# Attention, a mixture of experts and a feed-forward layer on one core: the route of five token tiles, the last gate, one V transfer and two narrowing operations change places

## The chip, the core and the metric

The kernel runs on one core of a Trainium2 chip. The metric is the device time of one execution in microseconds; the time of a kernel is the median of its runs. The profile is of one further execution.

## What is computed

Three layers follow one another in float32 (cut to what matters):

```python
scores = q @ k.T / 8 + bias            # 2 batches, 8 heads, 576 positions, head size 64
attn   = softmax(scores)               # bias: a small MLP of log-distances, per head
x      = (attn @ v) as [1152, 512]
logits = x @ w_gate;  e = argmax(logits);  gate = softmax(logits)[e]
# each token goes to its expert e; an expert takes the first 288 tokens in order
y      = gate * (relu(x @ w1[e]) @ w2[e])      # w1 [8,512,1024], w2 [8,1024,512]
h      = y @ w_in;  out = (h * cos(h)) @ w_out # [512,2048], [2048,512]
```

The kernel keeps float32 accuracy in the later layers by splitting each operand in a high and a low part, so that three matmuls stand for one. The weights of the last layer arrive as 64-bit numbers and are "narrowed" to float32 on the chip.

## The kernel before

**Attention.** The 1152 tokens are nine blocks of 128 rows: tiles 0 to 3 and 5 to 8, and one joint block for tiles 4 and 9 (64 rows of each batch). A block has four steps, one for each pair of heads, so there are 36 steps (`ns`), written out by `step_of(n)` (L882). In step n TensorE makes the scores of step n+1, transposes the exponentials of step n and multiplies those of step n-1 with V (`emit_pv`, L464); VectorE adds the bias to the scores of step n+1 (`emit_sum`, L411); ScalarE does the exponentials. The products are transposed back (`emit_nat`) and normalised into token rows (`emit_nrm`, L507) two steps later.

The bias is made in 36 groups, each by a few matmuls, an eviction, and a DMA (`bias_part`, L329) that spreads a group over the rows of a block's bias. Group n+10 is made in step n and sent in step n+1. The scores of step 8, summed in step 7, are the first of row block 1 and need its groups 8 to 15; group 15 is sent in step 6. The V pieces of batch 1 are loaded at the end of the steps listed in `V_AT` (L52, `load_step`, L839), one for each pair of heads; the last is first read by the values product of step 8. All these DMAs are issued from one queue, that of SyncE (SP), in the order of the code.

**Narrowing.** Each weight piece of the last layer needs one ScalarE operation and three on VectorE (shift, low, sign; `narrow`, L761); the last of them also issues the fetch of a later piece. `LOWS` (L40) says how many of the VectorE ones each late step takes.

**Gate and route.** When a block is done, `finish_block` (L538) makes its gate in four parts: f1 four matmuls (and a ScalarE or VectorE copy), f2 a transposition and the VectorE operations down to the expert's one-hot row `oh`, f3 an exponential on ScalarE, f4 the gate's value, a memset and an iota on GpSimd. `route(ts)` (L607) counts with small matmuls of the one-hot rows where each token of the tiles `ts` goes, then on VectorE makes the addresses `sl`, and GpSimd scatters the token rows into a buffer in DRAM (`disp`), one indirect DMA for each tile. Tiles 0 to 2 are routed during attention, tiles 3 to 7 in one call, tiles 8 and 9 last (`last_route`). The result of the counting lies where `late_ps` (L530) says.

**Expert 0** begins within step 35. `expert(s, ...)` (L1035) is a generator over eight groups m of the hidden layer:

```python
for k in range(4): ... T.matmul(out=ps, ...)      # 12 matmuls of the first layer, group m
for f in turn.get(m, ()): f()
...                                               # hh, hl, and splits of later weights (L1045 to L1050)
yield
for f in mid.get(m, ()): f()
if m > 0: second(s, m - 1)                        # 12 matmuls of the second layer, group m - 1
for f in side.get(m, ()): f()
```

Work of other parts is hung into `turn`, `mid` and `side` by hand. In the kernel before, `turn[1]` holds `last_but_one` (the transposition and normalisation of step 34), `mid[2]` holds `last_pair` (route of tiles 3 to 7, its matmuls around the same for step 35), `side[1]` the last block's f1, `side[2]` f2 to f4, `side[3]` `last_route` and `second_expert`, the DMA that fetches the second expert's rows from `disp` into `xg` and so waits for all scatters. The lists also hold the fetches of the second expert's weights. The next expert begins with `turned(1)`: TensorE transposes `xg`. Each engine works through its own instructions in the order of the code.

Of the kernel before, what the change touches and what calls it, by code (L numbers as in the profile page):

```python
# [24 lines left out]
E, FF, CAP = 8, 1024, 288  # L25
# [14 lines left out]
LOWS = {27: 1, 28: 2, 29: 2, 30: 1, 31: 1, 32: 2, 35: 3}  # L40
# [6 lines left out]
LATE_FROM = 32  # L47
# [1 line left out]
LATE_B = {34: 1}  # L49
LATE_C = {33: 1, 34: 1, 35: 1, 36: 1}  # L50
FETCH_AT = 1, 2, 4, 5
V_AT = 1, 3, 4, 5  # L52
CHOOSE = (1, 1)

LEAD = 10
# [52 lines left out]
def attention_moe_kernel(  # L108
# [116 lines left out]
    xb, bb, t0, t1 = (banks.tile([128, 512], F32, name=n) for n in ("xb", "bb", "t0", "t1"))  # L225
# [202 lines left out]
    def turn_half(ps, src, r):  # L428

        half = slice(64 * r, 64 * r + 64)  # L430
        T.transpose(ps, src[half], ident[half, half])  # L431
# [63 lines left out]
    def emit_nat(n):  # L495

        b, ib, p = steps[n]
        src = xs_t[b, ib][:, p, :]
        if at_step[0] < PLAIN:
            nat_t[n] = s_of[0][:, :, HS:HS + 64]  # L500
            for r in range(2):
                turn_half(nat_t[n][:, r], src, r)
        else:
            T.transpose(spare[0], src, ident)
            nat_t[n] = two_of(spare[0])

    def emit_nrm(n):  # L507
        b, ib, p = steps[n]
        ps = nat_t.pop(n)
        rz = rz_t[b, ib][:, 2 * p:2 * p + 2]  # L510
        V.tensor_tensor(
            out=xn_t[b, ib][:, 128 * p:128 * p + 128].rearrange("p (h d) -> p h d", h=2), in0=ps,
            in1=rz[:, :, None].to_broadcast([128, 2, D]), op=ALU.mult,
        )
# [10 lines left out]
    own = []  # L525
# [7 lines left out]
    def whole(f):  # L533

        for _ in f() or ():
            pass
# [200 lines left out]
    def go_on(rest_):  # L737
        for g in rest_:
            next(g, None)
# [99 lines left out]
    def load_step(n):  # L839
# [4 lines left out]
        if n == 2:  # L844
            Y.dma_start(out=wgs, in_=wg)
        if n in V_AT:
            load_v(1, (V_AT.index(n),))

# [30 lines left out]
    early_mags, early_lows = [f[0] for f in early_ops], [g for f in early_ops for g in f[1:]]  # L879
    ready, behind = [], []  # L880

    def step_of(n):  # L882

        g, nxt = RUNS.get(n), RUNS.get(n + 1)
        at_step[0] = n
        if n > 1:
            b, ib, p = steps[n - 2]
            if p == NP - 1 and n < SOONER:
                finish_block(b, ib)
                ready.append((b, ib))  # L890

        while ready and n >= ROUTE_FROM:
            tile_done(*ready.pop(0))
        while late and n < LATE_FROM and late[0][0] == -2:
            whole(late.pop(0)[1])
        if 0 < n <= PLAIN:
            emit_exp(n, 1)
        while behind:
            behind.pop(0)()
        if n in MAGS:  # L900
            early_mags.pop(0)()
        hook(n, "first")
        if n + 1 < ns:
            b, ib, p = steps[n + 1]
            j = BLOCKS.index((b, ib))
            for u in range(2):
                emit_qk(n + 1, u)
            if p == int(j == 1) and 0 < j < len(BLOCKS) - 1:
                fetch_q(*BLOCKS[j + 1])
            if n == 0:  # L910
                bias_h(g, quads=(3,))
            emit_exp(n + 1, 0)
        if n == ns - 4:
            aux[0] = V
        hook(n, "start")
        emit_tr(n)
        if n > 1:
            emit_nat(n - 2)
        hook(n, "turned")
        begun = []  # L920
        if n >= PLAIN:
            go_on(run_late(LATE_A.get(n, 0)))
            begun = run_late(LATE_B.get(n, n < LATE_FROM))
        emit_tev(n, 2)
        if g is not None:
            bias_half(g, 0)()
        emit_tev(n, 0)
        emit_tev(n, 1)
        if n < PLAIN:
            begun = run_late(1)  # L930
        e_t.pop(n)
        if nxt is not None:
            bias_h(nxt, quads=(0, 1))
        go_on(begun)
        if n > 1:
            emit_nrm(n - 2)
        if nxt is not None:
            bias_h(nxt, quads=(2, 3))
        for _ in range(LOWS.get(n, 0)):
            early_lows.pop(0)()  # L940
        while held:
            held.pop(0)()
        hook(n, "values")
        if 0 < n:
            emit_rz(n - 1)
            emit_pv(n - 1)
            if PLAIN <= n < ns - 1:
                emit_exp(n + 1, 1)
            emit_xs(n - 1)
        if n == SOONER:  # L950
            b, ib, p = steps[n - 1]
            finish_block(b, ib)
            tile_done(b, ib)
        go_on(run_late(LATE_C.get(n, 0)))
        if g is not None:
            evict = bias_half(g, 1, bb if n > 1 else xb[:, 128:])
            if g == NG - 1:
                evict()
            else:
                behind.append(evict)  # L960
        if n != ns - 2:
            made_up()
        load_step(n)
        while again and again[0][0] <= n:
            fetch_piece(again.pop(0)[1])
        if n in FILL_AT:
            i = FILL_AT.index(n)
            fill_rows(256 * i, min(256, E1 * CAP - 256 * i))
        if 0 <= n - DOUBLE_AT < NP:
            double(n - DOUBLE_AT)  # L970
        for j, at_ in enumerate(OUT_AT):
            if at_ == n:
                fill_out(j)
        hook(n, "end")
# [53 lines left out]

    def last_but_one():
        spare[0] = t1[:, 384:512]  # L1030
        emit_nat(ns - 2)
        emit_rz(ns - 1)
        emit_nrm(ns - 2)

    def expert(s, side, mid={}, turn={}):  # L1035

# [35 lines left out]
    e0_side, e0_mid = {m: [] for m in range(8)}, {}  # L1072
# [32 lines left out]
    emit_xs(ns - 1)  # L1105

    def last_pair():
        g = route(range(3, 8))()
        next(g)
        emit_nat(ns - 1)  # L1110
        emit_nrm(ns - 1)
        go_on([g])

    spare[0] = xb[:, 384:512]
    at_step[0] = ns
# [22 lines left out]
    def ids_of(i):  # L1138
        words = (xg if i < 2 else xs_few[:, None])[:, :, DM].bitcast(I32)
        V.tensor_copy(idn[i][0:words.shape[0], 0:words.shape[1]], words)  # L1140

    def ids_on(i, at_, o):
        n, c = (FEW, 1) if i == 2 else (96, 3)
        for j in range(c):
            T.transpose(xb[0:1, at_ + n * j:at_ + n * j + n], idn[i][0:n, j:j + 1], ident[:n, :n])
        A.activation(out=idrow[:, o], in_=xb[0:1, at_:at_ + n * c], func=AF.Copy)
# [105 lines left out]
        e0_side[m] += [in_e0.pop(0) for _ in range(n)]  # L1252
    f1, f2, f3, f4, last_route = [lambda f=f: whole(f) for f in tail]
    for m, fs in (
        (1, [f1]), (2, [f2, f3, f4]), (3, [last_route, second_expert]), (4, [make_list]), (5, [pick_few]),
    ):
        e0_side[m][0:0] = fs
    e0_mid.update({1: [lambda: ids_of(0)], 2: [last_pair], 6: [lambda: ids_on(0, 128, slice(0, CAP))]})
    for m, (a, c) in enumerate((((0,), (0,)), ((1,), ()), ((), (1,)), ((2,), ()), ((), (2,)), ((3,), (3,)))):
        e0_side[m] += [lambda a=a: fetch_w1(eid[1], a), lambda c=c: fetch_w2(eid[1], c)]  # L1260
    e0_side[6].append(fetch_third)
# [311 lines left out]
```

## Time and profile before

| what | value |
|---|---|
| median of 3 runs | 359.8 us (358.77, 359.80, 360.05) |
| the profiled execution, its own time | 361.18 us |
| its span in the profile | 359.4 us |
| TensorE matmuls busy | 343.7 us, 96% |
| VectorE, ScalarE, GpSimd busy | 82%, 74%, 11% |
| mean granted clock of TensorE | 0.984 of full speed |

All times in rows count from the start of the span. PE is TensorE's matmuls, PEld its weight loads, DVE VectorE, ACT ScalarE, POOL GpSimd, SP SyncE. "out<-in" are the program's tiles (numbers left out: `t` is t0 or t1, `v` v12); wo and wi also lend their room to other data, so `wo` can be the last V piece, a token row or a bias group on its way, and `wi` a V piece or the joint block's bias. In brackets stands how long an engine was idle before the instruction, and what the profile takes for the releaser.

### The profile page before, as it was taken

Reading aid. Unit: us, or ns where it says so; the run is one execution under the profiler, and the core shown is the slowest. Engines: PE = TensorE matmul, PEld = TensorE weight load, DVE = VectorE, ACT = ScalarE, POOL = GpSimd, SP = SyncE. Lnnn points to the kernel's source line nnn. Section 1 sums busy time; section 2 is a strip of 40 time slices with the busy share of each in tenths; the row PEclk is TensorE's granted clock in tenths of the full one; section 3 lists DMA queues with packets and bytes.
Section 4 is the critical chain, followed back from the end, with each engine's and each line's share of the span. In section 5 each row is a group of like instructions: output and inputs, shape, how many; then the busy total and the mean of one; then the engine's idle time right before and its main releaser. Section 6 shows DMA issues by size and latency. Waiting matters only on the chain.

```text
span 359.4 us, 10904 instructions
## 1 busy us (share of the span) xinstructions
PE 343.7 (96%) x4291; PEld 275.5 (77%) x4291; DVE 293.5 (82%) x770; ACT 267.7 (74%) x630; POOL 38.4 (11%) x89
## 2 busy tenths in 40 slices
PE   8989997999999999999999799999999999999992
PEld 6446775777666777777889799978898898898881
DVE  5998785898979987988989879977997887878550
ACT  6879995999988898999844478577877576766660
POOL 3000010010101420210006211300000000000023
PEclk9999998999999999999999989999999999999997
DMA  7799995786986697899348497954233133300003
GB/s 234 194 242 263 217 246 168 234 222 155 279 247 178 215 260 190 258 262 303 96 134 285 106 370 250 289 195 155 57 120 118 64 120 113 118 1 2 0 28 118
DMA packets 47021, 63.85 MB, mean 178 GB/s; under 512 B 5772, under 2 KB 30476, under 8 KB 46962
## 3 DMA queue, kind: packets, MB, share of 16 engines
q1 hardware_dynamic: 45666, 60.24, 57.5%
q0 software_dynamic: 1152, 2.48, 2.0%
q8 instruction: 35, 0.57, 0.7%
q10 hardware_dynamic: 144, 0.36, 0.3%
q14 instruction: 24, 0.20, 0.2%
HBM read 41.08 MB, written 11.47 MB: 146 GB/s over the span
## 4 chain that ended last, share of the span: by engine, by line
PE 44%; issue 29%; DVE 8%; ACT 5%; DMA 4%; POOL 1%; SPq 0%; POOLq 0%; DVEq 0%; ACTq 0%
PE sa L473 8%; PE bb L350 8%; PE hp L1042 5%; PE sb L406 5%; PE t L431 4%; PE sa L406 3%; PE t L1022 2%; DVE e L414 2%; ACT e L423 2%; PE sb L431 1%; DMA xg<-disp 1%; PE bb L1022 1%; PE ac L1022 1%; ACT et L454 1%; POOL out_dram L1389 1%
## 5 line engine op out<-in xcount | busy, mean ns | idle before, releaser
L423 ACT ACTIVATE e<-e,mn 128x576 f32<-128x576 f32 x72 | 56.3, 782 | 16.5 <-DVE mn L414 16.4
L324 DVE TENSOR_SCALAR h<-tt,sml 128x576 f32<-128x576 f32 x121 | 56.9, 515 | 0.1
L454 ACT ACTIVATE et<-t 128x512 f32<-128x512 f32 x72 | 38.9, 597 | 0.0
L350 PE MATMUL bb<-h,sml 128*32 128x288 f32 x400 | 35.5, 420 | 0.1
L431 PEld LDWEIGHTS t<-ident,e 64*128 64x128 f32 x576 | 24.2, 139 | 8.1 <-issue 1.8
L406 PE MATMUL sb<-k,q 64*128 64x288 f32 (+1 forms) x160 | 27.1, 449 | 1.1 <-DVE mn L414 1.0
L1305 PE MATMUL t<-yh,s1h 128*128 128x352 f32 (+1 forms) x88 | 26.8, 305 | 0.0
L1305 PE MATMUL t<-yh,s1l 128*128 128x352 f32 (+1 forms) x88 | 26.7, 303 | 0.0
L1305 PE MATMUL t<-yl,s1h 128*128 128x352 f32 (+1 forms) x88 | 26.5, 302 | 0.0
L431 PE MATMUL t<-ident,e 64*128 64x64 f32 x576 | 25.6, 225 | 0.8 <-ACT e L423 0.8
L356 ACT ACTIVATE wo<-bb,sml 128x288 f32<-128x288 f32 x49 | 24.8, 505 | 0.9 <-PE bb L350 0.8
L406 PE MATMUL sa<-k,q 64*128 64x288 f32 (+1 forms) x160 | 23.7, 405 | 0.0
L1426 ACT ACTIVATE gh<-tn 128x608 fp32r<-128x608 f32 (+2 forms) x19 | 12.0, 631 | 15.1 <-DVE tn L1423 15.0
L473 PE MATMUL sa<-et,wi 128*32 128x128 f32 (+1 forms) x700 | 23.0, 266 | 0.0
L406 PEld LDWEIGHTS sb<-k,q 64*128 64x128 f32 (+1 forms) x160 | 10.5, 174 | 16.2 <-issue 6.2
L1416 DVE TENSOR_TENSOR tn<-tn,kn 128x608 f32<-128x608 f32 (+2 forms) x19 | 13.1, 692 | 11.1 <-ACT kn L1413 11.1
L473 PEld LDWEIGHTS sa<-et,wi 128*32 128x32 f32 (+1 forms) x700 | 19.7, 114 | 2.4 <-DVE mn L414 1.5
L1042 PE MATMUL hp<-xh,s1h 128*128 128x288 f32 x64 | 19.8, 309 | 0.2 <-DVE xl L1016 0.2
L1401 PE MATMUL hp<-s2h,gh 128*128 128x512 f32 x48 | 19.1, 398 | 0.0
L1042 PE MATMUL hp<-xl,s1h 128*128 128x288 f32 x64 | 19.1, 298 | 0.0
L1401 PE MATMUL hp<-s2l,gh 128*128 128x512 f32 x48 | 19.0, 396 | 0.0
L1042 PE MATMUL hp<-xh,s1l 128*128 128x288 f32 x64 | 19.0, 297 | 0.0
(309 smaller groups left out, 993.5 us busy)
## 6 DMA issues: line engine op xcount, KB each, us to landing
keep<-win SPq DMA_DIRECT2D x16, 512.0 KB, 7.0
keep<-wout SPq DMA_DIRECT2D x16, 512.0 KB, 3.5
w1r<-mw SPq DMA_DIRECT2D x12, 512.0 KB, 5.2
w2r<-mw SPq DMA_DIRECT2D x12, 512.0 KB, 7.1
disp<-wo SPq DMA_DIRECT2D x10, 516.0 KB, 6.2
bias<-wo SPq DMA_DIRECT2D x15, 288.0 KB, 5.3
q<-qd SPq DMA_DIRECT2D x8, 512.0 KB, 6.8
k<-kd SPq DMA_DIRECT2D x8, 288.0 KB, 8.2
```

Of the source, the lines that this page charges most:

```text
L324: V.tensor_scalar(out=h, in0=win_, scalar1=col, scalar2=0.0, op0=ALU.add, op1=ALU.max)
L350: T.matmul(out=ps[32 * j:32 * j + 32, :], lhsT=w2s, rhs=h_t[g, j][:, cols], start=True, stop=True)
L356: A.activation(out=ev_t[g][:, cols], in_=ps, func=AF.Copy, scale=rst[:, g:g + 1])
L406: T.matmul(out=ps[a:e, half, 0:HS], lhsT=qt[b, ib][rows_, h, a:e], rhs=kt[c, p][rows_, u, :], start=True, stop=True)
L423: A.activation(out=e_t[n][:, u], in_=e_t[n][:, u], func=AF.Exp, scale=-1.0, bias=mn_t[n][:, u:u + 1], accum_out=z_t[b, ib][:, h:h + 1],)
L431: T.transpose(ps, src[half], ident[half, half])
L454: A.activation(out=et_t[n][:, 0:8, 64 * g:64 * g + 64], in_=halves[g], func=AF.Copy)
L473: T.matmul(out=xo[w * i:w * i + w], lhsT=v_of(c, p, at_, w), rhs=et[:, 4 if j == 4 else 5 * u + j, a:e], start=(j == 4), stop=(j == 3),)
L1022: T.matmul(out=acc[d], lhsT=a[g % 3][:, 128 * d:128 * d + 128], rhs=x[m % 2], start=(m == 0 and i == 0), stop=(m == 7 and i == 2),)
L1042: T.matmul(out=ps, lhsT=a[g % 3][:, k], rhs=x[:, k], start=(k == 0 and i == 0), stop=(k == 3 and i == 2))
L1305: done.append(T.matmul(out=sums(f, i), lhsT=w[f % 3][:, k], rhs=ya[k][x][:, o0 + a:o0 + e], start=(k == 0 and n == 0), stop=(k == 3 and n ...
L1401: T.matmul(out=oacc[t][rows_of(t)], lhsT=x, rhs=b[f % 3], start=(f == 0 and n == 0), stop=(f == 15 and n == 2))
```

## The change

The route of tiles 3 to 7 moves from `last_pair` in group 2 to `last_but_one` in group 1, around the latter's transposition, and its counts go to columns 128 to 256 of bank t1. What is left of `last_pair` moves from `mid[2]` to `side[1]`. f2 to f4 of the last block, its route and the fetch of the second expert's rows move from behind the second-layer product of their group to ahead of it. The last V piece of batch 1 is loaded at the end of step 6 and no more of step 5. In step 32 the two narrowing operations on VectorE come ahead of the normalisation of step 30.

```diff
--- before.py
+++ after.py
@@ -49,7 +49,7 @@
 LATE_B = {34: 1}
 LATE_C = {33: 1, 34: 1, 35: 1, 36: 1}
 FETCH_AT = 1, 2, 4, 5
-V_AT = 1, 3, 4, 5
+V_AT = 1, 3, 4, 6
 CHOOSE = (1, 1)
 
 LEAD = 10
@@ -878,6 +878,10 @@
     early_ops = [narrow(i) for i in range(EARLY)]
     early_mags, early_lows = [f[0] for f in early_ops], [g for f in early_ops for g in f[1:]]
     ready, behind = [], []
+
+    def narrow_on(n):
+        for _ in range(LOWS.get(n, 0)):
+            early_lows.pop(0)()
 
     def step_of(n):
 
@@ -932,12 +936,14 @@
         if nxt is not None:
             bias_h(nxt, quads=(0, 1))
         go_on(begun)
+        if n == LATE_FROM:
+            narrow_on(n)
         if n > 1:
             emit_nrm(n - 2)
         if nxt is not None:
             bias_h(nxt, quads=(2, 3))
-        for _ in range(LOWS.get(n, 0)):
-            early_lows.pop(0)()
+        if n != LATE_FROM:
+            narrow_on(n)
         while held:
             held.pop(0)()
         hook(n, "values")
@@ -1028,9 +1034,14 @@
 
     def last_but_one():
         spare[0] = t1[:, 384:512]
+        own.append(t1[:, 0:384])
+        g = route(range(3, 8))()
+        next(g)
         emit_nat(ns - 2)
         emit_rz(ns - 1)
         emit_nrm(ns - 2)
+        go_on([g])
+        own.pop()
 
     def expert(s, side, mid={}, turn={}):
 
@@ -1105,11 +1116,8 @@
     emit_xs(ns - 1)
 
     def last_pair():
-        g = route(range(3, 8))()
-        next(g)
         emit_nat(ns - 1)
         emit_nrm(ns - 1)
-        go_on([g])
 
     spare[0] = xb[:, 384:512]
     at_step[0] = ns
@@ -1252,10 +1260,10 @@
         e0_side[m] += [in_e0.pop(0) for _ in range(n)]
     f1, f2, f3, f4, last_route = [lambda f=f: whole(f) for f in tail]
     for m, fs in (
-        (1, [f1]), (2, [f2, f3, f4]), (3, [last_route, second_expert]), (4, [make_list]), (5, [pick_few]),
+        (1, [f1, last_pair]), (4, [make_list]), (5, [pick_few]),
     ):
         e0_side[m][0:0] = fs
-    e0_mid.update({1: [lambda: ids_of(0)], 2: [last_pair], 6: [lambda: ids_on(0, 128, slice(0, CAP))]})
+    e0_mid.update({1: [lambda: ids_of(0)], 2: [f2, f3, f4], 3: [last_route, second_expert], 6: [lambda: ids_on(0, 128, slice(0, CAP))]})
     for m, (a, c) in enumerate((((0,), (0,)), ((1,), ()), ((), (1,)), ((2,), ()), ((), (2,)), ((3,), (3,)))):
         e0_side[m] += [lambda a=a: fetch_w1(eid[1], a), lambda c=c: fetch_w2(eid[1], c)]
     e0_side[6].append(fetch_third)
```

## Rows read from the trace of the kernel before

**Rows 1.** The page: busy time of TensorE, and its granted clock in 40 slices.
```profile
PE 343.7 (96%) x4291; PEld 275.5 (77%) x4291; DVE 293.5 (82%) x770; ACT 267.7 (74%) x630; POOL 38.4 (11%) x89
...
PEclk9999998999999999999999989999999999999997
```

**Rows 2.** Windows: stretch, length, busy time by engine, granted clock, DMA share, GB/s.
```profile
45.00:50.00 5.00, 5.00 (x112) 3.88 (x108) 4.31 (x14) 4.39 (x13) 0.00 (x0) 1.00 1.10 250
57.70:61.10 3.40, 3.40 (x54) 2.48 (x50) 2.67 (x9) 2.70 (x9) 0.00 (x0) 0.50 1.00 289
207.90:211.30 3.40, 3.40 (x17) 3.40 (x16) 3.40 (x10) 2.80 (x8) 0.00 (x0) 0.50 1.08 370
```

**Rows 3.** Waits of TensorE, 5 to 64 us: total, times, longest.
```profile
PE sb L431 <- DVE mn L414: 2.3, 1, 2.3
```

**Rows 4.** TensorE's instructions in order of time: start, length, line, operation, idle before.
```profile
23.17 0.76 PE L406 MATMUL sb<-k,q 64*128 64x288 f32 x4 [0.97 <-DVE mn L414]
...
63.45 1.28 PE L473 MATMUL sa<-et,wo 128*32 128x128 f32 x40
...
181.21 0.40 PE L1022 MATMUL t<-hh,s2h 128*128 128x288 f32 x1
...
187.87 0.33 PE L556 MATMUL xb<-ident,wo 128*128 128x128 f32 x1 [0.40 <-DVE jk L634]
...
189.62 0.30 PE L1022 MATMUL t<-hh,s2h 128*128 128x288 f32 x1
...
206.56 0.93 PE L1011 MATMUL hp<-ident,xg 96*128 96x96 f32 x9 [1.85 <-DMA xg<-disp]
```

**Rows 5.** VectorE in order of time: the first sum of step 7.
```profile
56.13 0.76 DVE L414 CUSTOM_DVE_ANT_0 e<-sb,bias 128x576 f32<-128x576 f32 x1 [2.65 <-DMA wi<-wo]
```

**Rows 6.** SP's queue in order of time: the last V piece, bias group 15.
```profile
46.06 0.58 SPq L301 DMA_DIRECT2D wo<-vp  x1
...
49.73 0.53 SPq L331 DMA_DIRECT2D bias<-wo  x1
```

**Rows 7.** DMA issues from 20 to 60 us: count, KB each, median us to landing.
```profile
bias<-wo SPq DMA_DIRECT2D x8, 288.0 KB, 6.6
...
v<-vp SPq DMA_DIRECT2D x2, 320.0 KB, 10.3
```

**Rows 8.** VectorE's instructions in order of time, step 32 and expert 0.
```profile
163.91 0.29 DVE L511 TENSOR_TENSOR wo<-xb,rz 128x128 f32<-128x128 f32 x1 [1.02 <-ACT et L457]
...
181.29 0.45 DVE L1046 SCALAR_TENSOR_TENSOR hl<-hp,hh 128x288 fp32r<-128x288 f32 x1
...
185.69 0.46 DVE L1046 SCALAR_TENSOR_TENSOR hl<-hp,hh 128x288 fp32r<-128x288 f32 x1 [0.89 <-ACT hh L1045]
...
187.62 0.19 DVE L634 TENSOR_TENSOR jk<-xb,oh 128x40 f32<-128x40 f32 x1
...
189.17 0.22 DVE L559 TENSOR_TENSOR lp<-xb,rz 128x64 f32<-128x64 f32 x1
...
190.41 0.23 DVE L574 TENSOR_SCALAR oh<-eio,idxf 128x8 bf16<-128x8 f32 x1
...
194.47 0.16 DVE L646 SCALAR_TENSOR_TENSOR sl<-idxf,ov 128x2 int32<-128x2 f32 x1
...
205.42 0.69 DVE L985 TENSOR_TENSOR s1l<-w1r,s1h 128x512 fp32r<-128x512 f32 x1
```

**Rows 9.** Windows of line 614 alone: the route's 20 matmuls.
```profile
185.00:185.57 0.57, 0.53 (x20) 0.53 (x20) 1.00 0.00 0
```

**Rows 10.** GpSimd in order of time: first and last of the five scatters.
```profile
190.05 1.06 POOL L649 DMA_INDIRECT disp<-wo,sl  x1 [11.13 <-DVE top L567]
...
195.25 1.19 POOL L649 DMA_INDIRECT disp<-wo,sl  x1 [0.30 <-issue]
```

**Rows 11.** The chain that ended last, in order of time: start, length, what.
```profile
198.74 2.88 DMA disp<-wo,sl
...
201.80 4.63 DMA xg<-disp
```

## Prediction

> **What bounds the kernel now.** I read the page first, for the engine that fills the span; then the granted clock by stretches; then TensorE's waits; then, around the two long ones, the queues of the other engines. On the page TensorE is busy 96% of the span [rows 1], so a microsecond counts only where TensorE is idle or slow, and there the windows show something: two stretches of 3.4 us at a clock of 0.50 (the 1.2 GHz level), at 57.7 and at 207.9 [rows 2]. Both follow the two longest idle times of TensorE: 2.3 us in step 7 [rows 3], where the transposes wait for VectorE, and 1.85 us at 206.56 [rows 4], ahead of the second expert's first transposes. On the page's clock line they are the two eights (a slice is 9.0 us). An idle time of 0.97 us ahead of 23.17 and one of 0.40 ahead of 187.87 [rows 4] lie in slices that show a nine, which a stretch of 3.4 us at 0.50 would not leave. So a long stop costs itself and 1.7 us more (3.4 us of work at half speed), and one of a microsecond costs only itself.
>
> **The stop in step 7.** VectorE's sum for step 8 sat idle 2.65 us until 56.13 [rows 5]. The profile names a DMA into wi; but the sum reads the bias of row block 1, whose last group left at 49.73, the last V piece ahead of it at 46.06 [rows 6]. Such bias transfers land after 6.6 us in the median [rows 7]: 56.3, which is the time of the sum. I take that transfer for the releaser.
>
> **The change part by part. One V piece later.** The piece is 320 KB [rows 7]. It now leaves in step 6, behind the bias group, so the group's transfer has 320 KB less ahead of it. Between 45 and 50 us the DMA moved 250 GB/s [rows 2], so this is 1.3 us; TensorE's stop falls from 2.3 to 1.0 us. The bounds are 0 (the engine that lands last had no part of it queued) and 2.3 (the whole stop); the size over the measured rate is the nearest. The Trainium skill (DMA: Bandwidth & Descriptors, Specifications) gives some 358 GB/s as the HBM limit of a core. At that rate, as an estimate from that page, the piece would be 0.9 us, and the gain 0.4 smaller; the row shows less than that rate, and the row decides.
>
> A stop of 1.0 us is next to the one of 0.97 that left the clock alone, far from 1.85, so I take the half-speed stretch as gone: 1.7 us more (bounds 0 and 1.7). The step gains 1.3 + 1.7 = 3.0 us. The cover of the moved piece: it leaves at about 50.4, two V pieces of this size took 10.3 us in the median, which is 60.7; its first reader is the values product that began at 63.45 [rows 4], and would begin at 60.5. By the bias transfers' 6.6 us it is there at 57.0. I cost it at 0 (bounds 0 and 0.2). On SP's queue only the fill of the dispatch buffer behind it is issued half a microsecond later; nobody reads that buffer before the experts.
>
> **Narrowing ahead in step 32.** Two VectorE operations move in front of one normalisation. VectorE had idled 1.02 us there [rows 8], which now holds them; its next sums, and one weight piece's DMA on SP behind them, may come 0.6 us sooner. TensorE did not wait there: 0 (bounds 0.2 lost, if the later normalisation were awaited, and 0.6 gained).
>
> **Route of tiles 3 to 7 sooner.** Nothing is removed; 20 small matmuls (0.53 us [rows 9]), nine VectorE operations and five scatters move from behind the third first-layer group to behind the second. On TensorE the 0.53 is paid earlier and saved later. On VectorE the operations took from 187.62 to 189.17, 1.55 us; they now stand ahead of the operation that began at 181.29 [rows 8]. Everything behind is pushed by 1.55 us until the idle 0.89 us at 185.69 is used up; from there it is 0.66 late (0.95 with the last pair's normalisation, some 0.29 as at 163.91, which comes forward too), and, once past the old places of both, 0.89 early. Late in between are the narrowing of one piece (whose next fetch on SP, and four weight fetches queued behind it, leave up to 1.6 us later; the first split that reads them stands at 205.42 [rows 8]) and two weight splits that TensorE wants microseconds later. The route's sums now lie in bank t1, which the second output of expert 0's first product overwrites: TensorE began that product at 181.21 [rows 4] and begins it 0.53 later, when VectorE's read, 0.2 us from 181.3 on, is over. So I take 0; the bound above is the 0.40 us that the same kind of wait cost at 187.87 [rows 4], which this change removes, as the bank is another.
>
> GpSimd: the first scatter began at 190.05, 0.9 us after the addresses were there (189.2), and the five stand 1.30 us apart [rows 8, 10]. They now run from 183.7 to 190.2. A memset that stood ahead of them and the last tile's memset and iota come behind, with 4 us to do it in.
>
> **Last gate and route one product sooner.** On VectorE the order of these against the splits stays the same, so they come 0.89 us early and no more: the one-hot rows, done at 190.64 before, at 189.75; the addresses of tiles 8 and 9, done at 194.63 before, at 193.7 [rows 8]. On TensorE the last five route matmuls now stand in front of the second-layer product that began at 189.62 [rows 4]. TensorE comes there at 189.2 (0.40 us of waiting gone) and waits 0.6 for the one-hot rows: a new wait, with that product and all of the expert queued behind it. Net cost 0.2 us (bounds: 0.4 gained and 1.5 lost, if VectorE gains nothing there).
>
> What it buys: GpSimd was the late one, with the seventh scatter at 198.74 [rows 11]. Now it waits for the addresses: 193.7 + 0.9 + 1.3 = 195.9, 2.8 us sooner. The fetch of the second expert's rows, issued at 201.80 after the last scatter had landed and 4.63 us in the air [rows 11], lands at 203.6 instead of 206.4. On SP it passes nothing; the five weight fetches behind it go 2.8 us sooner as well. TensorE is done with expert 0 at 204.7 + 0.2. The stop of 1.85 us is gone with 1.3 us to spare, and with it the half-speed stretch. This part: 1.85 - 0.2 + 1.7 = 3.35 us. Late next would be VectorE's xl operations, which follow a split done at 206.1 [rows 8]; but TensorE first has the last second-layer product of expert 0 to do, after transposes that begin at 204.9. I take 0 there (bounds 0 and the 0.7 of that split). That TensorE keeps a gain from there on is read off its 96%.
>
> **The sum** is 3.0 + 3.35 = 6.3 us. The profiled execution took 361.18 us, so 354.9. The median of the three other runs is 1.4 us lower (359.8), near the cost of one half-speed stretch. If they have both, the change gives 353.5; if they lack one, it gives them 4.6 and 355.2. I take 354.3.
>
> **The rivals**, against the median. (1) The profile's name for the releaser in step 7 is right, and the sum waits for the DMA into wi. Moving the V piece then gives nothing: 6.3 - 3.0 = 3.3, so 356.5. For it: the row's words. Against it: the sum does not read that tile.
>
> (2) The new wait in front of the second-layer product takes the place of the old one. If VectorE brings the one-hot rows no sooner than before, TensorE waits 1.4 us, and if that lowers the clock, 1.7 go as well. The second part is then 1.85 - 1.0 - 1.7 + 1.7 = 0.85, the whole 3.9: 355.9; with the fetch late as well, 3.0 and 356.8.
>
> (3) Neither stop goes: the slowest of the DMA engines lands the bias group as late as before, and the row fetch is bound by its 4.63 us behind scatters that land late. 359.8, no change.
>
> (4) Slower: the V piece, now behind everything, lands after its reader. The product that would begin at 60.5 waits; past 1.85 us the clock falls as well. It takes back the 6.3 us from a landing 15 us after issue on, and one of 17 us costs 6.9 + 1.7 - 6.3 = 2.3: 362.1. The longest median in that stretch is 10.3 [rows 7], which speaks against it.
>
> **How the numbers follow.** Forecast 0.64, rival (1) 0.14, (2) 0.10, (3) 0.08, (4) 0.04. The three runs shown spread by 1.28 us, so about 0.5% (1.8 us) is what can be told from no change. Faster by more is the forecast with (1) and (2), 0.88; within it (3), 0.08; slower (4), 0.04. The range goes from 352.4 (353.5 less the idle 1.0 us in step 7, were it to go whole, rounded) to 357.2 (the worse form of (2), with 0.4 for the wait at bank t1).
>
> **What would show it.** Right: TensorE's wait in step 7 near 1.0 us and the clock at 1.00 after it; the fetch of the second expert's rows issued near 196 in the new time (199.0 less the 3.0 gained before); no TensorE wait for it; in its place about 0.6 us ahead of the last route matmuls; one half-speed stretch only, that of the last slice [rows 1]. Wrong: a stretch at 0.50 anywhere between 50 and 250 us, or a wait of over 1.5 us in expert 0.

## Result and profile after

The changed kernel took 355.1 us (median of 4 runs, 354.62 to 356.39) against 359.28 us of the kernel before beside it (4 runs, 358.77 to 360.05): ratio 0.9887, 95% interval [0.9852, 0.9923]. That is faster by 4.2 us. Forecast were 354.3 us in a range of 352.4 to 357.2. Its profiled execution took 354.73 us, with a span of 353.0 us. The first profile of the kernel before, from which the prediction was read, is of a slow execution: 361.18 us at a mean granted clock of 0.984, where the changed kernel's has 0.997.

The page of the changed kernel, the lines of [rows 1]:

```profile
PE 340.7 (97%) x4291; PEld 272.8 (77%) x4291; DVE 294.1 (83%) x770; ACT 267.5 (76%) x630; POOL 37.8 (11%) x89
...
PEclk9999999999999999999999999999999999999998
```

The two eights of the kernel before are gone: TensorE keeps its full clock (2.4 GHz) up to the last slice. Of its waits for other engines, those from 171 to 202 us, the last steps of attention and expert 0, are (the waits view, columns as in [rows 3]):

```profile
PE xb L556 <- DVE wo L511: 0.6, 1, 0.6
PE xb L504 <- ACT wo L552: 0.4, 1, 0.4
PE hp L1053 <- DVE xl L1022: 0.2, 1, 0.2
```

From 30 to 66 us there is none at all, where [rows 3] had 2.3 us. The wait for the second expert's rows (1.85 us in [rows 4]) is gone too. The first two lines are new. (`xb` and `t1` are banks of PSUM, which holds TensorE's results in this kernel.)

The instructions of the changed kernel in order of time, SP, VectorE, GpSimd and TensorE (the lines 1011 to 1046 of the kernel before are 1017 to 1057 here):

```profile
50.42 0.58 SPq L301 DMA_DIRECT2D wo<-vp  x1
...
53.81 0.76 DVE L414 CUSTOM_DVE_ANT_0 e<-sb,bias 128x576 f32<-128x576 f32 x1 [0.22 <-PE sb L406]
...
159.97 0.69 DVE L778 SCALAR_TENSOR_TENSOR wi<-keep,wi 128x512 int32<-128x512 int32 x1
160.58 0.28 DVE L511 TENSOR_TENSOR wo<-xb,rz 128x128 f32<-128x128 f32 x1
...
178.70 0.17 DVE L646 SCALAR_TENSOR_TENSOR sl<-idxf,ov 128x5 int32<-128x5 f32 x1
...
187.60 0.46 DVE L1057 SCALAR_TENSOR_TENSOR hl<-hp,hh 128x288 fp32r<-128x288 f32 x1 [1.30 <-ACT hh L1056]
...
191.07 0.16 DVE L646 SCALAR_TENSOR_TENSOR sl<-idxf,ov 128x2 int32<-128x2 f32 x1
...
179.65 1.11 POOL L649 DMA_INDIRECT disp<-wo,sl  x1 [24.37 <-DVE hl L1057]
...
185.05 0.97 POOL L649 DMA_INDIRECT disp<-wo,sl  x1 [0.30 <-issue]
...
192.02 1.05 POOL L649 DMA_INDIRECT disp<-wo,sl  x1 [5.15 <-DVE hl L1057]
193.38 0.98 POOL L649 DMA_INDIRECT disp<-wo,sl  x1 [0.30 <-issue]
...
195.84 0.34 SPq L159 DMA_DIRECT2D xg<-disp  x1
...
180.30 0.33 PE L504 MATMUL xb<-ident,wo 128*128 128x128 f32 x1 [0.40 <-ACT wo L552]
...
182.85 0.33 PE L556 MATMUL xb<-ident,wo 128*128 128x128 f32 x1 [0.64 <-DVE wo L511]
...
186.20 0.18 PE L614 MATMUL xb<-oh,tri 128*128 128x8 bf16 x1
...
201.13 0.91 PE L1017 MATMUL hp<-ident,xg 96*128 96x96 f32 x9
```

The V piece leaves at 50.42, behind the bias, and the first sum of step 7 waits for TensorE's scores and for no DMA [rows 5]. The five early scatters run from 179.65 to 186.02 and no more from 190.05 to 196.4 [rows 10]. The fetch of the second expert's rows is issued at 195.84, not 201.80 [rows 11], and TensorE transposes them at 201.13 without a wait. Part of that is a general shift: expert 0 begins at 171.01 instead of 175.07. Counted from there, the fetch is 1.9 us sooner. VectorE stands idle for 1.30 us at 187.60, waiting for ScalarE, ahead of the addresses of tiles 8 and 9 (`sl` at 191.07), and GpSimd's last two scatters, idle for 5.15 us, wait for them.

### The profile page after: what moved, and what is told of

Same layout as the page of the kernel before. It is cut to its first block, busy times and chain, and to the rows that moved or that the text cites. A ratio compares the mean times of both kernels' runs of the same rounds, so it can differ in the third digit from the quotient of the medians.

```text
span 353.0 us, 10902 instructions
## 1 busy us (share of the span) xinstructions
PE 340.7 (97%) x4291; PEld 272.8 (77%) x4291; DVE 294.1 (83%) x770; ACT 267.5 (76%) x630; POOL 37.8 (11%) x89
## 4 chain that ended last, share of the span: by engine, by line
PE 43%; issue 30%; DVE 12%; ACT 3%; POOL 1%; DMA 1%; SPq 0%; POOLq 0%; DVEq 0%; ACTq 0%
PE sa L473 8%; PE bb L350 8%; PE sb L406 5%; PE hp L1053 4%; PE t L431 4%; PE sa L406 3%; PE t L1028 3%; DVE e L414 3%; PE sb L431 1%; PE bb L1028 1%; ACT e L423 1%; PE ac L1028 1%; DVE s1l L991 1%; POOL out_dram L1397 1%; DVE wi L775 1%
## 5 line engine op out<-in xcount | busy, mean ns | idle before, releaser
L1313 PE MATMUL t<-yh,s1l 128*128 128x352 f32 (+1 forms) x88 | 26.7, 303 | 0.0
L356 ACT ACTIVATE wo<-bb,sml 128x288 f32<-128x288 f32 x49 | 24.8, 505 | 0.8 <-PE bb L350 0.8
L473 PEld LDWEIGHTS sa<-et,wi 128*32 128x32 f32 (+1 forms) x700 | 19.6, 114 | 2.6 <-DVE mn L414 1.8
L1056 ACT ACTIVATE hh<-hp 128x288 fp32r<-128x288 f32 x16 | 6.5, 409 | 16.5 <-PE hp L1053 11.3
L1409 PE MATMUL hp<-s2h,gl 128*128 128x512 f32 x48 | 18.9, 394 | 0.0
```

Of the source, the lines that this page charges most:

```text
L356: A.activation(out=ev_t[g][:, cols], in_=ps, func=AF.Copy, scale=rst[:, g:g + 1])
L473: T.matmul(out=xo[w * i:w * i + w], lhsT=v_of(c, p, at_, w), rhs=et[:, 4 if j == 4 else 5 * u + j, a:e], start=(j == 4), stop=(j == 3),)
L1313: done.append(T.matmul(out=sums(f, i), lhsT=w[f % 3][:, k], rhs=ya[k][x][:, o0 + a:o0 + e], start=(k == 0 and n == 0), stop=(k == 3 and n ...
L1409: T.matmul(out=oacc[t][rows_of(t)], lhsT=x, rhs=b[f % 3], start=(f == 0 and n == 0), stop=(f == 15 and n == 2))
```

## Experiments

Three groups of four kernels, each group on one chip beside the kernel before, which took 358.0, 358.4 and 358.62 us in the median there (25, 22 and 19 runs). The last two columns are of each kernel's one profiled execution: TensorE's wait for VectorE's sum in step 7, and the length of expert 0, from its first first-layer matmul to the first transposition for the next expert. The ratio is the one on record; it is an estimate of its own and need not be the quotient of the two medians (for after_again that quotient, 355.35 / 358.62, is 0.9909).

| kernel | what differs | ratio, interval | step 7, us | expert 0, us |
|---|---|---|---|---|
| (before, first profile) | | 1 | 2.3 | 31.5 |
| (after, first profile) | | 0.9887 [0.9852, 0.9923] | 0 | 30.1 |
| before_again | nothing, the kernel before | 0.9999 [0.9972, 1.0025] | 0.7 | 32.2 |
| v_only | before, V piece later | 1.0009 [0.9978, 1.0040] | 0 | 32.3 |
| filled | before, matmuls in both gaps | 1.0086 [1.0052, 1.0119] | 0 | 33.3 |
| route_only | after, V piece back | 0.9902 [0.9866, 0.9938] | 2.2 | 30.4 |
| gates_back | after, last gate and route back | 0.9907 [0.9874, 0.9941] | 0 | 29.7 |
| pair_later | after, last pair one product later | 0.9928 [0.9897, 0.9959] | 0 | 30.1 |
| narrow_back | after, narrowing back | 0.9940 [0.9917, 0.9963] | 0 | 30.1 |
| twice | after, 4 more scatters early | 1.0015 [0.9988, 1.0042] | 0 | 32.0 |
| after_again | the changed kernel | 0.9894 [0.9864, 0.9923] | 0 | 30.2 |
| route_again | route_only again | 0.9893 [0.9861, 0.9925] | 0 | 30.1 |
| narrow_again | narrow_back again | 0.9937 [0.9907, 0.9966] | 0 | 30.4 |
| quiet | after, 4 more scatters late | 0.9962 [0.9933, 0.9990] | 0 | 30.2 |

None of the twelve profiles from before_again down shows a half-speed stretch ahead of the last slice. In filled, expert 0 includes the 30 added matmuls.

Four of the twelve profiles (before_again, narrow_again, twice, after_again) share a stop that comes with the change and without it: in step 32 TensorE stands still for 0.75 to 1.46 us in the middle of a row of values products, and the profile names no engine that it waited for. narrow_again has the longest:

```profile
162.02 0.73 PE L473 MATMUL bb<-et,wi 128*32 128x128 f32 x17 [1.46 <-issue]
```

Its cause is not shown. One profile can thus differ from the next by over a microsecond for a reason that is not under test.

### before_again: the kernel before once more

> The kernel before once more, for a second profile of it. My theory: the two stops of TensorE are there each time (the one for the second expert's rows 1.8 us within 0.2, the one in step 7 anywhere from 0.5 to 2.3 us, as the slowest DMA engine has it), but a half-speed stretch does not follow each of them in every execution; a profiled time under 360 us then shows at most one such stretch. Rival: both stretches and both stops are there at a time under 360 us as well, and the profiled execution of 361.18 us was longer for some other reason. Ratio 1.000 within 0.003 by both.

Measured: 358.0 us, 0.9999. Step 7 shows a wait of 0.7 us only, no half-speed stretch follows, and TensorE does not wait for the row fetch. Yet expert 0 is no shorter than in the first profile: the time is lost in another way. Its instructions in order of time, TensorE, ScalarE, VectorE:

```profile
193.22 0.18 PE L1161 MATMUL xb<-srun,ones 128*128 128x8 bf16 x1
...
194.79 0.30 PE L1042 MATMUL hp<-xh,s1l 128*128 128x288 f32 x1
...
203.87 0.40 PE L1022 MATMUL t<-hl,s2h 128*128 128x288 f32 x1 [0.69 <-DVE hl L1046]
...
205.90 0.96 PE L1011 MATMUL hp<-ident,xg 96*128 96x96 f32 x9 [0.45 <-DVE hl L1046]
...
198.78 0.41 ACT L1045 ACTIVATE hh<-hp 128x288 fp32r<-128x288 f32 x1 [4.40 <-PE hp L1042]
...
197.29 0.17 DVE L1162 COPY cnt<-xb 128x8 f32<-128x8 f32 x1 [2.10 <-PE ac L1022]
```

The matmuls of group 4 end at 194.79 + 0.30 = 195.09, and ScalarE's relu of their sums starts at 198.78, 3.7 us later. VectorE's copy reads a matmul of 193.22 and starts at 197.29. In the first profile of the kernel before the relu of this group started at 196.52, 0.03 us after the matmuls' end (196.19 + 0.30). So TensorE's results were taken up late here, and TensorE waited afterwards for VectorE's `hl`. v_only and filled show the same: relus up to 3.8 us late while the scatters run. This set the question for "twice". What the DMA engines did between the matmuls' end and the relu (columns as in [rows 2]):

```profile
195.09:198.78 3.69, 3.43 (x27) 3.09 (x26) 1.32 (x11) 0.00 (x0) 2.02 (x3) 1.00 0.08 23
```

GpSimd still issued scatters, but at a DMA share of 0.08 next to nothing else was moved.

### v_only: the V piece's move alone

```diff
-V_AT = 1, 3, 4, 5
+V_AT = 1, 3, 4, 6
```

> Only the V piece is moved, from step 5 to step 6. My theory: TensorE's wait in step 7 falls below 1.1 us, no half-speed stretch follows it, the wait of 1.8 us for the second expert's rows stays; 1.0 to 3.0 us less (ratio 0.992 to 0.997). Rival: the sum of step 7 waits for the DMA into wi; the wait of 2 us stays and the ratio is 1.000 within 0.002.

Measured: 358.27 us, 1.0009. The stop in step 7 is gone from the profile, as the theory had it, but the ratio is the rival's: the median does not move. By the lower end of the interval, 0.9978, the piece is worth 0.8 us at most, not 3.0.

### route_only: the change without the V piece's move

```diff
-V_AT = 1, 3, 4, 6        # from the changed kernel
+V_AT = 1, 3, 4, 5
```

> The change without the V piece (loaded at the end of step 5 as before). My theory: no wait for the second expert's rows, no half-speed stretch after 200 us, the wait in step 7 as in the kernel before; 1.6 to 3.3 us less than before (ratio 0.991 to 0.9955). Rival: the new waits in expert 0 take the place of the old one, ratio 0.998 to 1.002; then nearly all of the 4.2 us gained in the medians comes from the V piece.

Measured: 355.11 us, 0.9902: nearly the whole gain without the V piece, a little more than the theory's range. TensorE's wait from 40 to 64 us in its profile, and VectorE's first sum of step 7:

```profile
PE sb L431 <- DVE mn L414: 2.2, 1, 2.2
...
56.11 0.76 DVE L414 CUSTOM_DVE_ANT_0 e<-sb,bias 128x576 f32<-128x576 f32 x1 [2.56 <-DMA bias<-wo]
```

A stop of 2.2 us, as long as the 2.3 of [rows 3]; but the page's clock line shows nines up to the last slice, so no half-speed stretch follows. The length of the stop alone does not decide. The releaser named here is the bias transfer, which the prediction had taken it for.

### filled: the kernel before with TensorE kept busy in both gaps

```diff
+        if n == 7:        # ahead of the transposes of step 7; 30 more ahead of turned(1)
+            for _ in range(36):
+                T.matmul(out=xb[:, 384:512], lhsT=ones, rhs=ones, start=True, stop=True)
```

> The kernel before with TensorE kept busy where it stopped: 36 matmuls of 128 columns in step 7 ahead of the last transposes, 30 ahead of the second expert's transposes, into columns nobody reads. They take no wait away. My theory: the bias and the rows come as late as before, but the clock stays at 1.00 to the last slice, so 0 to 3.4 us less, as many stretches as there were: some 1.5 us (ratio 0.993 to 0.999). Rival: the stretches at 0.50 do not come from the idle time; they stay, and the ratio is 1.000 or, by the matmuls, up to 1.002.

Measured: 361.42 us, 1.0086, above both the theory's range and the rival's. In its profile the 36 matmuls take 2.18 us of step 7 and the 30 others 1.85 us. If a usual execution of the kernel before lost 1.7 us twice to a low clock, this kernel should have won; it lost 3 us. The mean granted clock, which is on record for every timed execution, says the same: over 78 of the kernel before (beside the three groups, and before_again) the median is 0.995 and the lowest 0.986, against 0.984 in the first profile. So an execution with both half-speed stretches of [rows 2] is rare. A single stretch would take about 0.005 off the mean (an estimate: 3.4 us at half speed in 359), so the eleven executions at 0.991 or lower may have had one.

### gates_back: last gate and route at their old place

```diff
-        (1, [f1, last_pair]), (4, [make_list]), (5, [pick_few]),
+        (1, [f1, last_pair]), (2, [f2, f3, f4]), (3, [last_route, second_expert]), (4, [make_list]), (5, [pick_few]),
...
-    e0_mid.update({1: [lambda: ids_of(0)], 2: [f2, f3, f4], 3: [last_route, second_expert], 6: [...]})
+    e0_mid.update({1: [lambda: ids_of(0)], 6: [...]})
```

> The changed kernel, but with the last gate's pieces (f2 to f4), the last route and the second expert's row fetch where they stood before, one product later each; the route of tiles 3 to 7, the V piece and the narrowing stay as changed. Theory (two losses sat in the first expert: the row fetch came too late for the second expert, and it is the whole move, scatters and last route together, that takes it away): the row fetch is issued about one step (3.3 us) later than the 195.84 us of the changed kernel's profile, lands near 203.7 us, and TensorE, there at 201.1, waits 2 to 3 us for it: ratio to the kernel before 0.994 to 0.998. Rival (it is the early scatters of tiles 3 to 7 alone that free the first expert): no wait for the rows over 0.7 us, ratio 0.987 to 0.992, as the changed kernel's 0.9887.

Measured: 355.35 us, 0.9907: the rival held. In order of time, SP and TensorE:

```profile
196.81 0.34 SPq L159 DMA_DIRECT2D xg<-disp  x1
...
201.65 0.93 PE L1017 MATMUL hp<-ident,xg 96*128 96x96 f32 x9 [0.29 <-DMA xg<-disp]
```

The fetch leaves 24.9 us after expert 0 began (171.94), in the changed kernel 24.8 (195.84 against 171.01), in the kernel before 26.7 (201.80 against 175.07). Moving the last gate and route brought the fetch nothing; with this part taken back, what is left to bring it forward is getting the five scatters out of the way. The move cost nothing either: the 0.64 us wait of the changed kernel is replaced by 0.29 us here.

### pair_later: the last pair one product later

```diff
-        (1, [f1, last_pair]), (4, [make_list]), (5, [pick_few]),
+        (1, [f1]), (2, [last_pair]), (4, [make_list]), (5, [pick_few]),
```

> The changed kernel, but the last pair's transposition and normalisation one product later, behind the next product of the first expert. Theory: the two new TensorE waits of the changed kernel's profile (0.40 us ahead of the last pair's transposition, for f1's copy out of the same bank, and 0.64 us ahead of f2's, for the last pair's normalisation) lose at least the first: with a product of 1.65 us between them f1's copy is done in time; if f2's wait stays, 0.4 us are won, if both go 1.0: ratio 0.986 to 0.988. Rival (VectorE, which is busy without a break from 177 to 186 us, sets the pace there): the waits move to f2 and grow by what is won, ratio as the changed kernel's 0.9887 or up to 0.4 us worse, 0.988 to 0.990.

Measured: 355.69 us, 0.9928, no better; the theory failed. The two waits became one (TensorE, in order of time):

```profile
185.38 0.33 PE L504 MATMUL xb<-ident,wo 128*128 128x128 f32 x1 [0.94 <-DVE lp L559]
```

The order in the code is now f2, then the last pair, and the last pair's transposition waits for VectorE's read of f2's sums. 0.94 us stand for 0.40 + 0.64, and expert 0 is as long as before. The waits come from one PSUM bank (`xb`) that takes turns, and from VectorE's place in its queue; shifting one product does not remove them.

### narrow_back and narrow_again: the narrowing at its old place

```diff
-        if n == LATE_FROM:
-            narrow_on(n)
         if n > 1:
             emit_nrm(n - 2)
...
-        if n != LATE_FROM:
-            narrow_on(n)
+        narrow_on(n)
```

> The changed kernel without the third part of the change: in step 32 the narrowing stands again behind the row-sum normalisation. Theory (the narrowing's place costs nothing, since VectorE has room in that step): ratio within 0.15 per cent of the changed kernel's 0.9887, so 0.987 to 0.9905. Rival (the 1.02 us that VectorE stood idle there before come back and reach the end): 1.0 us more, ratio 0.991 to 0.992.

> The changed kernel without the narrowing's move, beside the changed kernel itself. Theory (it costs and gains nothing): ratio within 0.2 per cent of the changed kernel's on this chip. Rival (the 1.0 us that VectorE idles in step 32 reaches the end): 0.25 to 0.5 per cent above.

Measured: 356.05 us, 0.9940, and on the third chip 356.37 us, 0.9937, where the changed kernel had 355.35 us, 0.9894. The intervals overlap, but both came out the same way, the rival's: on the one chip 0.43% or 1.5 us above the changed kernel by the ratios, 1.0 us by the medians. So the part that I had at 0 is most likely worth 1.0 to 1.5 us. narrow_back's VectorE and TensorE in order of time:

```profile
160.16 0.29 DVE L511 TENSOR_TENSOR wo<-xb,rz 128x128 f32<-128x128 f32 x1 [1.00 <-ACT et L457]
...
162.30 0.75 DVE L414 CUSTOM_DVE_ANT_0 e<-sb,bias 128x576 f32<-128x576 f32 x1
...
164.28 0.29 DVE L511 TENSOR_TENSOR wo<-xb,rz 128x128 f32<-128x128 f32 x1 [0.34 <-ACT et L457]
...
164.63 0.33 PE L556 MATMUL xb<-ident,wo 128*128 128x128 f32 x1 [0.45 <-DVE wo L511]
```

VectorE idles 1.00 us again at 160.16, its sum of step 33 starts at 162.30 (161.54 in the changed kernel, whose step began 0.2 us later), and TensorE's transposition for the gate waits 0.45 us for the normalisation at the end of that queue. v_only, with the old order as well, has 0.44 us there, the changed kernel none. That shows 0.5 us of it; where the rest sits stays open. narrow_again's profile does not help: its stop of 1.46 us in step 32 comes first, and behind it TensorE does not wait for the normalisation.

### twice: four of the early scatters issued again

```diff
                     sent.append(i_)
+                for i, t in list(enumerate(ts))[:4 if len(ts) == 5 else 0]:
+                    i_ = P.indirect_dma_start(out=junk[:, :], ...)   # same rows, same addresses
```

> The changed kernel with four of the five early scatters issued a second time, into a DRAM tensor that nobody reads, so that GpSimd goes on issuing scatters to about 191.5 us instead of 186. In three profiles of the kernel before on this chip ScalarE and VectorE took up TensorE's finished sums up to 3.8 us late (ScalarE's relu at 198.78 us for matmuls done at 195.1), always while the scatters ran. Theory (the scatters delay the signals that TensorE sends): such late starts show between 186 and 192 us, ScalarE's idle time ahead of a relu over 2.5 us with its matmuls long done, and the ratio goes up to 0.991 to 0.996. Rival (the lateness comes from something else, scatters by themselves cost GpSimd's time alone): the relus start within 0.7 us of their matmuls' end, ratio 0.987 to 0.9905.

Measured: 359.34 us, 1.0015, more than the theory's range. (The three profiles that the expectation speaks of are those of before_again, v_only and filled, on another chip.) Four scatters that nobody waits for cost the whole gain. In order of time, GpSimd, TensorE, ScalarE, VectorE:

```profile
188.09 0.97 POOL L661 DMA_INDIRECT junk<-wo,sl  x1 [0.30 <-issue]
...
192.36 0.97 POOL L661 DMA_INDIRECT junk<-wo,sl  x1 [0.30 <-issue]
...
190.53 0.30 PE L1063 MATMUL hp<-xh,s1l 128*128 128x288 f32 x1
...
194.17 0.41 ACT L1066 ACTIVATE hh<-hp 128x288 fp32r<-128x288 f32 x1 [3.77 <-remote]
...
194.61 0.46 DVE L1067 SCALAR_TENSOR_TENSOR hl<-hp,hh 128x288 fp32r<-128x288 f32 x1 [1.60 <-ACT hh L1066]
```

The relu starts at 194.17 for matmuls that ended at 190.83: 3.3 us late, as in the kernel before. Expert 0 is 32.0 us long instead of 30.1, about half of the 4 us lost. So with added scatters in that stretch the late take-up is back. The windows of the same profile say what else runs there (columns as in [rows 2]):

```profile
180.00:184.00 4.00, 3.05 (x29) 2.39 (x27) 3.93 (x10) 0.88 (x3) 2.59 (x3) 1.00 0.02 4
184.00:188.00 4.00, 4.00 (x34) 3.93 (x35) 3.15 (x13) 1.24 (x4) 3.17 (x3) 1.00 0.82 191
188.00:192.00 4.00, 4.00 (x33) 4.00 (x32) 2.48 (x8) 1.45 (x3) 3.31 (x3) 1.00 1.04 366
```

From 184 us on the second expert's weights are on their way, so here, other than in before_again, scatters and weights run together. The relus of the changed kernel, whose scatters are done at 186.02, start at most 0.8 us late (187.16, for matmuls that end at 186.35).

### quiet: the same four scatters behind the weights

```diff
+                for i, t in list(enumerate(range(3, 7))) if len(ts) == 2 and ts[0] == 8 else []:
+                    i_ = P.indirect_dma_start(out=junk[:, :], ...)   # behind the last route's two
```

> The changed kernel with the same four scatters into the unread tensor as in the run before, but issued behind the last route's two, from about 194.5 to 199.7 us, when the second expert's weights have landed (DMA share 0.04 from 194 to 196). Theory (TensorE's signals are late only where scatters and the weights' transfer run together): no relu starts more than 0.7 us after its matmuls' end before 198 us, ratio within 0.3 per cent of the changed kernel's. Rival (scatters alone delay the signals): relus 1.5 to 4 us late between 195 and 200 us, as with the scatters from 188 to 193, ratio 0.5 per cent or more above the changed kernel's.

Measured: 356.46 us, 0.9962, above the changed kernel's 0.9894 (the rival's ratio) but far below twice's 1.0015. Its twelve times lie in two bunches, 355.67 to 356.55 (seven) and 358.32 to 359.48 (five); the profiled execution is of the lower one. There the take-up is late by 0.9 us at most, a weight split of ScalarE:

```profile
195.38 0.63 ACT L1001 ACTIVATE s2h<-w2r 128x512 fp32r<-128x512 f32 x1 [0.99 <-PE ac L1040]
```

In the changed kernel the wait at this place is 0.32 us. So in the one execution that can be looked at, late scatters delay little. What the upper bunch lost was not seen, and the two theories are not told apart here; before_again, late at a DMA share of 0.08, speaks against a weight transfer at the same time as a condition.

### after_again and route_again: the V piece on one chip

> The changed kernel once more, as the common base of the three that follow. By its first comparison (0.9887) and those of the variants (0.9902 with the V piece at its old place, 0.9907 with the last gate and route at theirs, 0.994 with the narrowing at its) it is expected at 0.987 to 0.992. Where one part of the change is worth over 1 us by itself, the variant without it stands at least 0.3 per cent above this ratio on this chip.

> The changed kernel with the V piece back in step 5. Theory (the stop in step 7 that the V piece causes shows in profiled executions alone: with the piece in step 5 the profiled execution stood 1.4, 2.1 and 1.8 us above its kernel's median, with the piece in step 6 between 1.0 below and 0.5 above): the median is within 0.2 per cent of the changed kernel's on this chip, the profiled execution 1 us or more above it, with a TensorE stop of 1.5 to 2.5 us in step 7. Rival (the V piece's place is worth 1.3 us or more in every execution, as the prediction had it): the ratio stands 0.35 to 0.8 per cent above the changed kernel's.

Measured: 355.35 us, 0.9894, and with the V piece back 355.33 us, 0.9893. No gain from the V piece's place shows in the median. That the profiled execution would differ from the others, as I supposed, fell: route_again's took 355.1 us, 0.2 below its median, with no wait for VectorE in step 7 at all, and after_again's, with the piece in step 6, 357.26 us, 1.9 above. Over all profiles that wait shows in three of four kernels with the piece in step 5 (2.3, 0.7, 2.2 us and none; filled, whose matmuls cover the place, not counted) and in none of the nine with it in step 6. It is tied to the V piece, and still the medians do not show it. Why is open: the stop may be rare in timed executions, or made up later.

## Why the prediction was right, and which of its steps were not

The forecast held, 354.3 against 355.1 us, but that was partly luck: its sum came out by errors that partly cancelled. On the third chip the gain is 3.8 us by the ratio (0.0106 of 358.62), 3.3 by the medians. Undoing one part at a time there gives the V piece 0.0 and the narrowing 1.5 (1.0 by the medians); by subtraction 2.3 are left for the route with the last gate, which no run undoes together. The prediction had 3.0, 0 and 3.35.

- **What bounds the kernel: right in rule, wrong in size.** TensorE's idle time did set the pace. But "a long stop costs itself and 1.7 us more" was read off one execution. A stop of 2.2 us in route_only lowered no clock, and none of the three other profiles with the old route has the two stretches. Half of the sum (1.7 twice, of 6.3) thus stood on something that a usual execution does not have. The prediction's own hint was there: its profiled execution was 1.4 us above the median, and it allowed for one stretch missing, not for both.
- **One V piece later: the mechanism right, its worth wrong.** The bias transfer, with the V piece ahead of it, was what the sum waited for, and rival (1) (a DMA into `wi`) falls: with the piece moved, the sum waits for TensorE, and in route_only the profile names the bias transfer. The stop went whole, not by 1.3 us, so the place in the queue counted for more than the piece's size over the measured rate; what else it delays was not tried. The step failed in taking one execution's 2.3 us for what an execution loses: no loss there shows in the median. The Trainium skill's rate (DMA: Bandwidth & Descriptors, Specifications) gave 0.9 us, as an estimate, and the row's 1.3; the stop shrank by more than either, so no run decides between them. The cover held: no wait for V anywhere.
- **Narrowing ahead: costed at 0, worth 1.0 to 1.5 us.** The step named the right rows, the 1.02 us idle and "up to 0.6 gained" as a bound, and stopped at "TensorE did not wait there" in one profile. In that execution step 32 took 4.15 us from scores to scores, and the gate's transposition in step 33 did not wait; in narrow_back step 32 took 3.65, and the transposition waits 0.45. So a longer step 32 had hidden the wait. This is the largest mis-sized term in the other direction.
- **Route of tiles 3 to 7 sooner: right.** The first scatter came 8.6 us after the beginning of expert 0, as the working had it (183.7 against 175.07), and bank t1 cost nothing. By subtraction this move with the last gate is worth 2.3 us, against 3.35 less its 1.7 for the clock = 1.65. But what they bring is in part another thing than "GpSimd was the late one": in the three other profiles with the old route, all of one chip, expert 0 lost its 2 us to results taken up late while scatters ran, and the row fetch was not awaited.
- **Last gate and route one product sooner: no gain, and the wait at another place.** The sum expected 0.6 us ahead of the last route's matmuls. There is none at 186.20; TensorE waits 0.40 and 0.64 us earlier, where the last pair and the last gate share bank `xb` with f1. The working had looked for f2's one-hot rows and not for the bank under the transpositions that the same edit brings together. The 0.89 us that VectorE was to bring did not come: the addresses of tiles 8 and 9 were done 20.2 us after the beginning of expert 0 (191.23), in the kernel before 19.6 (194.63), as VectorE now idles 1.30 us at 187.60. gates_back shows that this part could be left out. The fetch left at 195.84, for "near 196", which is luck: from the beginning of expert 0 it was 0.9 us later than forecast (24.8 against 23.9), and expert 0 began 4.1 us sooner instead of 3.0.
- **The signs to look for** came out in the main: no stretch at 0.50, no wait for the row fetch, no wait over 1.5 us in expert 0. Two did not: the wait in step 7 was 0 and not near 1.0 us, and the 0.6 us ahead of the last route was missing. The signs could not show that two of the three prices were off; only undoing the parts one at a time did.

Rivals (2) to (4) did not occur: the new waits, 1.04 us in all, are less than the old ones and lower no clock, and no V piece came late.

## What to carry over

Before pricing a stop, look whether it is in more than one execution: here the pair of half-speed stretches was the profiled execution's own, and removing the longest stop did not move the median. Try GpSimd's indirect DMAs outside stretches in which ScalarE and VectorE wait closely on TensorE: moving five scatters 6 us ahead (the first from 15.0 to 8.6 us after the beginning of expert 0) was worth about 2 us by subtraction, and four useless ones cost about 4. An engine's idle time ahead of a small operation can be worth filling with work from behind it (here 1.0 to 1.5 us), even if no other engine waits there in the profile at hand.

## What the hardware showed unexpectedly

Results of TensorE were taken up to 3.8 us late while scatters ran: relu at 198.78 for matmuls that end at 195.09 (before_again, DMA share 0.08 in between), at 194.17 for 190.83 (twice, weights on their way), against 0.03 us in the kernel before's first profile, whose scatters ran as well. So scatters alone do not bring it about each time. The profile names TensorE or "remote" as the releaser. The Trainium skill (Perfetto Trace Analysis, Tensor Engine Instruction) says that a matmul's shown end is computed, and that its signal goes out only when PSUM has acknowledged the writes. By that page either the writes or the signal may have been late; no run here shows which, nor why one execution escaped it.

A stop of TensorE of 2.3 us was followed by 3.4 us at half the clock (1.2 GHz), one of 2.2 us in another execution by none.
